# Attention and a gated FFN on one core: weights decoded in pieces of 512 columns, the ninth transposed block in the scores' banks, scores ranked further ahead

## The chip, the cores and the metric

The kernel runs on one core of one Trainium2 chip. The metric is device time in microseconds. Before the change three runs took 1001.59 to 1005.19 us, with a median of 1004.27. The core has five engines that work side by side, each through its own instructions in their order: TensorE (PE in the profile), VectorE (DVE), ScalarE (ACT), GpSimd (POOL) and SyncE (SP), which issues the transfers. PE writes its results into PSUM, which has eight banks; each holds 512 float32 columns.

## What is computed

For 8 batches of 576 tokens, attention with 8 heads of 64 columns, in which scores more than tau under their row's maximum are dropped, and then an FFN whose hidden layer is gated by a convolution of three taps along the tokens:

```python
scores = scale * np.matmul(q, k.transpose(0, 1, 3, 2))
thresh = np.max(scores, axis=-1, keepdims=True) - tau
scores = np.where(scores >= thresh, scores, -1000000000.0)
attn = softmax(scores); x = np.matmul(attn, v)      # heads side by side: [8, 576, 512]
h = np.maximum(x @ w_in, 0.0)                       # [8, 576, 1024]
conv_out[:, s] = sum(conv_w[k] * h[:, s + k - 1] for k in range(3))
out = (h * 1.0 / (1.0 + np.exp(-conv_out))) @ w_out # [8, 576, 512]
```

The FFN's weights (w_in 512 x 1024, w_out 1024 x 512, conv_w 3 x 1024) come as 64-bit floats and are turned into pairs of 32-bit floats on the chip, a high and a low part.

## The kernel before

**Tiles.** A batch is worked on in two chunks: tokens 0 to 255 (query tiles 0 and 1 of 128 rows) and 256 to 575 (tiles 2 and 3 of 128 rows, tile 4 of 64). Heads go in pairs, four pairs a chunk. One query tile of one pair is a unit; in `unit` (L403) PE makes the scores of each head into a score buffer `ps_s` of two PSUM banks, 288 of 512 columns used in each (L423 for batch 0, in plain float32 and 64 rows; L434 for the others, with q and k split in high and low parts). DVE takes the row maximum (L443, `few`), ACT the exponential (L449, `em`), DVE masks and sums (L452), and after a few operations on single columns POOL normalises (L482). The 64-row tile has both heads in one buffer. There are two score buffers, so a batch makes 36 turns of them: 16 in its first chunk, 20 in its second.

`transposes` (L487) turns the two heads' 1152 columns in nine blocks of 128 on PE (L504): four, four and one, each group into a bank of `ps_t`, of which there are two, and ACT copies it out to `eT` (L498). The 64-row tile makes a group of four and one of two halves (L528). `attend` (L541) multiplies by v, also in a `ps_t` bank, and splits the result in a high part on ACT (L558) and a low one on DVE (L561). `mm1` (L567) and `mm2` (L636) are the FFN: 8 blocks of hidden columns per chunk (L580 on PE into `ps_w`; relu L595 on ACT, the taps L598 on POOL and L607 on DVE, the gate L616 and L614, and split into the ring `gh`, `gl` at L624 and L253), and output tiles of 128 tokens (L645). `ps_w` has two banks, which makes 4 + 2 + 2 = 8.

**Weights.** `split` (L268) decodes a piece of 128 rows and `WN` = 256 columns: a transfer on SP (L306), the absolute value of the upper words on ACT (L279), four operations on DVE (a clamp L283, a shift L287, then sign and low bits joined at L291 and L295), the high part by ACT (L298) and the low part by POOL (L253). There are 32 pieces, 16 for each weight, and they lie in the `ot` buffers, two in all. Batch 0's attention runs while they are decoded.

**What sets the order.** Nothing is issued directly. `op` (L64) records an operation with its engine, a planned duration, the parts of buffers that it reads and writes, and a rank: the number of the unit it belongs to, less `AHEAD` of its kind ('s' for the steps of `unit`, 't' for transposes, 'a' for attend, 'prep' for q, k and v, 'w' for weights, of which `WRATE` pieces are ranked per unit). FFN work has no lead. `Plan.run` (L82) then plays the program with the planned durations, and on each engine always takes the ready operation of lowest rank; on PE it may pass over some within `KEEP` ranks to avoid a change of kind. The order in which it takes them is the order of the program. The dependences that the plan knows are those of the named parts (`r=` and `w=`). The semaphores of the program are put in afterwards, by a layer that looks at what each instruction reads and writes: for PSUM it orders accesses to one tensor by bank.

Of the kernel before, what the change touches and what calls it, by code (L numbers as in the profile page):

```python
# [18 lines left out]
AHEAD = {'s': 4.5, 't': 4.0, 'a': 3.5, 'prep': 5.5, 'w': 2.0}  # L19
# [4 lines left out]
BACKLOG = {'pool': 10000.0, 'dve': 500.0, 'act': 9e9}  # L24
WRATE = (1.75, 1.25)
ALT = 3.0

# [6 lines left out]
KEEP = 0.6  # L34


class Buf:
# [6 lines left out]
    def __getitem__(self, key):  # L44
        if self.tile is None:
            self.tile = self.pool.tile(self.shape, self.dtype, tag=self.tag, bufs=self.bufs, name=self.name)
        return self.tile[key]

# [146 lines left out]
def tile_tau_attention_gated_ffn(  # L195
# [3 lines left out]
    kd: bass.AP,  # L199
    vc: bass.AP,  # L200
# [19 lines left out]
    GROUPS = [(0, 1), (2, 3, 4)]  # L220
    CHUNKS = [(0, 255), (255, 321)]
    COLS = [(0, 256), (254, 322)]
    NEW = [(0, 256), (256, 320)]
# [4 lines left out]
    ps_s = ctx.enter_context(tc.tile_pool(name="ps_s", bufs=2, space=PSUM))  # L228
# [11 lines left out]
    op("sp", 100, lambda: nc.sync.dma_start(tau_sb[:], tau.broadcast_to([P, 1])), w=[(tau_sb, 0)], ahead=100.0)  # L240

# [26 lines left out]
    def split(src, n, name, high, low, hr, lr):  # L268


        tmp = plan.buf(wk, "ot", 2, [P, 3 * WN], U32, name)

        def view(dtype=F32):
            words = tmp[:, :2 * n].rearrange("p (f two) -> p f two", two=2)
            return [x.bitcast(dtype) for x in (words[:, :, 0], words[:, :, 1], tmp[:, 2 * n:3 * n])]

        def f1():
            lo, hi, a = view()
            nc.scalar.activation(a, hi, AF.Abs)  # L279

        def f2():
            a = view()[2]
            nc.vector.tensor_scalar(a, a, TINY, None, op0=ALU.max)  # L283

        def f3():
            a = view(U32)[2]
            nc.vector.tensor_scalar(a, a, 3, 0x3FFFFFF8, op0=ALU.logical_shift_left, op1=ALU.bitwise_and)  # L287

        def f4():
            lo, hi, a = view(U32)  # L290
            nc.vector.scalar_tensor_tensor(a, hi, 0xC0000000, a, op0=ALU.bitwise_and, op1=ALU.bitwise_or)  # L291

        def f5():
            lo, hi, a = view(U32)
            nc.vector.scalar_tensor_tensor(a, lo, 29, a, op0=ALU.logical_shift_right, op1=ALU.bitwise_or)  # L295

        def f6():
            nc.scalar.activation(high(), view()[2], AF.Copy)  # L298

        def f7(engine):  # L300
# [481 lines left out]
```

## Time and profile before

| what | value |
| --- | --- |
| median of three runs | 1004.27 us |
| the profiled execution's own time | 1007.23 us |
| its span, first to last instruction | 1005.4 us |
| mean granted PE clock | 0.974 |
| busy: PE, DVE, POOL, ACT | 948.6, 816.0, 725.6, 706.4 us |
| transfers | 77.76 MB, mean 77 GB/s |

The page has busy times for the whole span, and these hide stages. It also has the span in forty slices; other views group instructions by line and form (busy time, mean duration of one, idle time before them and who ended it), list who waited for whom (us in total, how often, the longest), and give each engine's busy time in chosen stretches. A row's mean duration includes what the instruction lost to its neighbours on the chip. PE's matmuls overlap, so its busy time is not the sum of their durations.

### The profile page before, as it was taken

The numbers are of one execution on the slowest core, as the hardware profiler recorded it, in microseconds if no ns is written. First come the engines' busy times: TensorE is split into PE (matmuls) and PEld (weight loads), VectorE is DVE, ScalarE is ACT, GpSimd is POOL, SyncE is SP. The second block draws the span as 40 slices with busy tenths as digits, with TensorE's granted clock in tenths as the row PEclk, the third lists the DMA queues.
The fourth block names the chain that finished last, engine by engine and source line by source line (L and its number), as shares of the span: only waits on it lengthen the run. The fifth ranks groups of instructions, "written<-read, shape, count | busy, mean of one in ns | idle before, by whom it ended". The sixth has DMA issues, their size and how long they took to land.

```text
span 1005.4 us, 19531 instructions
## 1 busy us (share of the span) xinstructions
PE 948.6 (94%) x6368; PEld 769.7 (77%) x6368; DVE 816.0 (81%) x2023; ACT 706.4 (70%) x1575; POOL 725.6 (72%) x1157
## 2 busy tenths in 40 slices
PE   6788777999999999999999999999999999999998
PEld 3455455778888788878888888887788888887796
DVE  5889998887887967898788877898789877897543
ACT  5576676777777776777777777678776776776543
POOL 3567787687677978697776978698766886696433
PEclk9796997999999999999999999999999999999999
DMA  6434342223221233222312232213322121211000
GB/s 172 127 104 128 102 125 80 76 62 97 83 71 51 78 91 90 66 65 81 109 57 65 64 100 71 81 36 102 100 75 63 53 82 57 70 47 38 22 22 32
DMA packets 47172, 77.76 MB, mean 77 GB/s; under 512 B 5600, under 2 KB 23008, under 8 KB 47072
## 3 DMA queue, kind: packets, MB, share of 16 engines
q1 hardware_dynamic: 47072, 76.53, 26.0%
q8 instruction: 51, 0.84, 0.4%
q14 instruction: 49, 0.40, 0.1%
HBM read 67.07 MB, written 9.44 MB: 76 GB/s over the span
## 4 chain that ended last, share of the span: by engine, by line
PE 74%; DVE 8%; POOL 8%; issue 3%; ACT 3%; DMA 3%; SPq 1%; POOLq 0%; ACTq 0%; DVEq 0%
PE po L645 18%; PE ph L580 16%; PE ps_s L434 13%; PE pa L550 13%; PE ps_t L504 12%; POOL em L482 2%; POOL gl L253 2%; DVE few L443 2%; DVE em L452 2%; PE ps_s L423 1%; DMA stage<-in_w_out_dram 1%; DVE t L607 1%; POOL t L598 1%; ACT eT L498 1%; POOL ks L253 1%
## 5 line engine op out<-in xcount | busy, mean ns | idle before, releaser
L482 POOL TENSOR_SCALAR em<-em,few 128x576 f32<-128x576 f32 x288 | 259.6, 908 | 44.1 <-DVE few L477 30.5
L443 DVE TENSOR_REDUCE few<-ps_s 128x1 f32<-128x576 f32 x288 | 213.2, 750 | 67.2 <-PE ps_s L434 51.6
L580 PE MATMUL ph<-x,w1h 128*128 128x322 f32 (+1 forms) x1024 | 254.5, 311 | 1.3 <-ACT hp L595 1.0
L452 DVE SCALAR_TENSOR_TENSOR em<-ps_s,few,em 128x576 f32<-128x576 f32 x288 | 231.6, 810 | 28.6 <-ACT em L449 24.3
L449 ACT ACTIVATE em<-ps_s,few 128x576 f32<-128x576 f32 x288 | 211.8, 742 | 52.2 <-DVE few L443 43.7
L498 ACT ACTIVATE eT<-ps_t 128x512 f32<-128x512 f32 (+1 forms) x448 | 200.0, 479 | 53.7 <-PE ps_t L504 50.2
L504 PE MATMUL ps_t<-ident,em 128*128 128x128 f32 x1280 | 204.1, 282 | 18.9 <-POOL em L482 12.0
L504 PEld LDWEIGHTS ps_t<-ident,em 128*128 128x128 f32 x1280 | 154.5, 144 | 62.2 <-POOL em L482 30.1
L434 PE MATMUL ps_s<-ks,q 128*128 128x288 f32 (+1 forms) x1120 | 193.6, 307 | 6.0 <-DVE em L452 6.0
L607 DVE SCALAR_TENSOR_TENSOR t<-hp,cw,t 128x255 f32<-128x255 f32 (+1 forms) x256 | 172.7, 681 | 23.9 <-POOL t L598 20.1
L580 PEld LDWEIGHTS ph<-x,w1h 128*128 128x128 f32 x1024 | 180.1, 192 | 10.0 <-issue 3.5
L434 PEld LDWEIGHTS ps_s<-ks,q 128*128 128x128 f32 (+1 forms) x1120 | 161.1, 186 | 18.5 <-DVE em L452 6.8
L550 PE MATMUL pa<-eT,v 128*64 128x256 f32 (+1 forms) x1280 | 172.9, 417 | 1.0 <-ACT eT L498 1.0
L580 PE MATMUL ph<-x,w1l 128*128 128x322 f32 (+1 forms) x512 | 153.0, 299 | 0.1
L253 POOL TENSOR_TENSOR gl<-t,gh 128x321 fp32r<-128x321 f32 (+13 forms) x184 | 119.5, 659 | 36.0 <-ACT gh L624 33.8
L550 PEld LDWEIGHTS pa<-eT,v 128*64 128x64 f32 x1280 | 87.8, 139 | 69.8 <-issue 7.1
L645 PE MATMUL po<-w2h,gh 128*128 128x512 f32 x288 | 121.2, 421 | 2.5 <-ACT w2h L298 1.9
L645 PE MATMUL po<-w2l,gh 128*128 128x512 f32 x288 | 113.7, 395 | 0.8 <-POOL w2l L253 0.8
L645 PE MATMUL po<-w2h,gl 128*128 128x512 f32 x288 | 113.2, 393 | 0.4 <-POOL hp L590 0.3
L253 POOL TENSOR_TENSOR q<-xq,q 128x256 fp32r<-128x256 f32 (+1 forms) x112 | 93.9, 844 | 18.1 <-ACT q L391 16.8
L598 POOL TENSOR_SCALAR t<-hp,cw 128x321 f32<-128x321 f32 (+1 forms) x128 | 70.6, 553 | 45.6 <-ACT hp L595 40.5
L580 PEld LDWEIGHTS ph<-x,w1l 128*128 128x128 f32 x512 | 98.2, 192 | 0.9 <-POOL w1l L253 0.3
(54 smaller groups left out, 1115.8 us busy)
## 6 DMA issues: line engine op xcount, KB each, us to landing
v<-in_vc_dram SPq DMA_DIRECT2D x64, 320.0 KB, 2.9
out_dram<-ot SPq DMA_DIRECT2D x36, 256.0 KB, 2.1
xk<-in_kd_dram SPq DMA_DIRECT2D x28, 320.0 KB, 3.0
xq<-in_qd_dram SPq DMA_DIRECT2D x56, 160.0 KB, 2.2
xk<-in_kd_dram SPq DMA_DIRECT2D x28, 288.0 KB, 2.9
xq<-in_qd_dram SPq DMA_DIRECT2D x56, 128.0 KB, 2.1
stage<-in_w_in_dram SPq DMA_DIRECT2D x16, 256.0 KB, 3.1
stage<-in_w_out_dram SPq DMA_DIRECT2D x16, 256.0 KB, 2.6
```

The costliest lines, as they stand in the source:

```text
L253: engines[e].tensor_tensor(dst, x, y, op=ALU.subtract)
L434: nc.tensor.matmul(ps[:(r + 1) * n, c, :CH], lhsT=qt[j][i][:, o - r * n:o + n], rhs=kt[j][:, at:at + CH], start=(i == 0), stop=(i == 1))
L443: nc.vector.tensor_reduce(few[:rows, nm], ps[:rows, :, :CH], op=ALU.max, axis=mybir.AxisListType.XY, negate=True)
L449: nc.scalar.activation(view(), ps[:rows, :, :CH], AF.Exp, bias=few[:rows, nm])
L452: nc.vector.scalar_tensor_tensor(view(), ps[:rows, :, :CH], few[:rows, th], view(), op0=ALU.is_ge, op1=ALU.mult, accum_out=few[:rows, total])
L482: engines[e].tensor_scalar(sl, sl, few[:rows, 6 + h:7 + h], few[:rows, 8 + h:9 + h], op0=ALU.mult, op1=ALU.add)
L498: "act", act(w, True), lambda dst=dst, src=src: nc.scalar.activation(dst(), src(pt), AF.Copy),
L504: nc.tensor.transpose(out=pt[:, i * P:(i + 1) * P], in_=em[:, (b0 + i) * P:(b0 + i + 1) * P], identity=ident[:])
L550: nc.tensor.matmul(pa[j * D:(j + 1) * D, :w], lhsT=vt[:, blk + j, :], rhs=eT[:, blk, :w], start=(r == 0), stop=(r == 4))
L580: nc.tensor.matmul(ph[:, :an], lhsT=w1[w][:, cb, fs], rhs=xs[cb][:, h, :an], start=(cb == 0 and i == 0), stop=(cb == NCB - 1 and i == 2))
L607: nc.vector.scalar_tensor_tensor(t[:, :kn], hp[:, k:kn + k], cw[:, 3 * f + k:3 * f + k + 1], t[:, :kn], op0=ALU.mult, op1=ALU.add)
L645: nc.tensor.matmul(po[:], lhsT=x[:, f, at:at + P], rhs=w[:, f, :], start=(f == 0 and i == 0), stop=(f == NFB - 1 and i == 2))
```

## The change

- **Weights.** `WN` is 512: 16 pieces, 8 for each weight. The 64-bit words land in one of four buffers shared with the keys (`ks`), the values in one of two shared with the low parts of q (`q2`). The clamp goes to POOL, with DVE as the other choice; DVE keeps three operations. The first three loads are issued by ACT's queue, at the program's start. `WRATE` is 0.99 and 0.812 pieces a unit.
- **Odd blocks.** The ninth block of a tile, and the two halves of the 64-row tile, go into the last 128 columns of a bank of a score buffer, units alternating over the two buffers and then over their banks. The two score buffers are now made once and stay; the planner keeps a part's name for the scores and one for each bank's free columns, so to the plan the two uses are independent.
- **Order.** `AHEAD` is 6.0 for scores (4.5), 3.25 for transposes (4.0), 4.5 for prep (5.5), 3.0 for weights (2.0), and a load of weights has 5.5 more; `KEEP` is 1.2 (0.6). The first output tile's products are ranked with chunk 0's.
- **Smaller ones.** Batch 0's keys come for both heads of a pair in one transfer of 128 rows x 640 columns, loaded again for the second chunk, and scaled by one ACT operation. ACT's table is loaded by a first exponential of a column of zeros at the program's start. Later keys of both heads lie in one buffer, `ks`, four in all.

```diff
-AHEAD = {'s': 4.5, 't': 4.0, 'a': 3.5, 'prep': 5.5, 'w': 2.0}
+AHEAD = {'s': 6.0, 't': 3.25, 'a': 3.5, 'prep': 4.5, 'w': 3.0, 'load': 5.5}
-WRATE = (1.75, 1.25)
+WRATE = (0.99, 0.812)
+EARLY = 1
-KEEP = 0.6
+KEEP = 1.2
...
+    warm = const("warm", [P, 1], F32)
+    op("pool", 100, lambda: nc.gpsimd.memset(warm[:], 0.0), w=[(warm, 0)], ahead=200.0)
+    op("act", 1300, lambda: nc.scalar.activation(warm[:], warm[:], AF.Exp), w=[(warm, 0)], ahead=200.0)
...
-    def split(src, n, name, high, low, hr, lr):
-        tmp = plan.buf(wk, "ot", 2, [P, 3 * WN], U32, name)
+    def split(src, n, name, high, low, hr, lr, queue="sp"):
+        stage = plan.buf(wk, "ks", 4, [P, KW], U32, name)
+        value = plan.buf(wk, "q2", 2, [P, 2, QW], U32, f"{name}_f")
...
-        def f2():
-            a = view()[2]
-            nc.vector.tensor_scalar(a, a, TINY, None, op0=ALU.max)
+        def f1(e):
+            engines[e].tensor_scalar(v(), v(), TINY, HUGE, op0=ALU.max, op1=ALU.min)
...
+        op(queue, 450, load, w=[hi, lo], ahead=w + (AHEAD["load"] if queue == "sp" else 90))
+        op("act", act(n), f0, w=[a], r=[hi], ahead=w)
+        op("pool", n * 1.69 + 80, f1, w=[a], ahead=w, other=[("dve", 150 + n * 0.65)])
+        op("dve", 150 + n * 0.55, f2, w=[a], ahead=w)
+        op("dve", 150 + n * 1.1, f3, w=[a], r=[hi], ahead=w)
+        op("dve", 150 + n * 1.1, f4, w=[a], r=[lo], ahead=w)
...
-    WN = 256
+    WN = 512
...
+    scores = [plan.buf(ps_s, f"ps_s{i}", 1, [P, 2, 512], F32, f"ps_s{i}") for i in range(2)]
+    taken = collections.Counter()
+    def turns(what, n):
+        taken[what] += 1
+        return (taken[what] - 1) % n
...
+        op("sp", 450, lambda: nc.sync.dma_start(ks[:], kp[p]), w=[(ks, 0)], ahead=a + 2)
+        op("act", act(S + D), lambda: nc.scalar.activation(ks[:], ks[:], AF.Copy, scale=0.125), w=[(ks, 0)], ahead=a)
...
-            ps = plan.buf(ps_s, "ps_s", 2, [P, 2, 512], F32, f"ps_s_{u}_{h}")
+            ps = scores[turns("s", 2)]
...
-            pt = plan.buf(ps_t, "ps_t", 2, [P, 512], F32, f"ps_t_{u}_{i}")
             width = sum(w for w, _, _ in evacs)
+            if width > P:
+                pt = plan.buf(ps_t, "ps_t", 2, [P, 512], F32, f"ps_t_{u}_{i}")
+                part, bank = (pt, 0), lambda: pt
+            else:
+                at = turns("t", 4)
+                pt, half = scores[at % 2], at // 2
+                part, bank = (pt, 1 + half), lambda: pt[:, half, 512 - P:]
```

**DVE, the weights in batch 0.** Rows of DVE's order in batch 0's first chunk before the change, where two pieces of w_in (`stage`) stand between the maximum of a head and the masks of its unit (`few` holds the columns of maxima, limits and sums, `em` the exponentials):

```order
L443 TENSOR_REDUCE few_319<-ps_s_1_340 128x1
L283 TENSOR_SCALAR stage_286<-stage_286 128x256
L283 TENSOR_SCALAR stage_310<-stage_310 128x256
L287 TENSOR_SCALAR stage_286<-stage_286 128x256
L287 TENSOR_SCALAR stage_310<-stage_310 128x256
L291 SCALAR_TENSOR_TENSOR stage_286<-stage_286 128x256
L291 SCALAR_TENSOR_TENSOR stage_310<-stage_310 128x256
L295 SCALAR_TENSOR_TENSOR stage_286<-stage_286 128x256
L295 SCALAR_TENSOR_TENSOR stage_310<-stage_310 128x256
L452 SCALAR_TENSOR_TENSOR em_350,few_319<-ps_s_0_306,few_319,em_350 128x576
```

And DVE's order in the same chunk after it (`stage_105` the words of a piece, `stage_f` the values; `ps_s_127` and `ps_s_136` are the two score buffers from here on):

```order
L473 TENSOR_REDUCE few_303<-ps_s_127 128x1
L473 TENSOR_REDUCE few_303<-ps_s_136 128x1
L476 TENSOR_SCALAR few_303<-few_303,tau_sb 128x1 x2
L325 SCALAR_TENSOR_TENSOR stage_f<-stage_105,stage_f 128x512
L482 SCALAR_TENSOR_TENSOR em_319,few_303<-ps_s_127,few_303,em_319 128x576
L482 SCALAR_TENSOR_TENSOR em_319,few_303<-ps_s_136,few_303,em_319 128x576
L328 SCALAR_TENSOR_TENSOR stage_f<-stage_105,stage_f 128x512
L507 RECIPROCAL few_303<-few_303 128x2
```

Between a unit's last maximum and its first mask stood eight operations of 256 columns, and now one of 512; the pieces' operations are spread between those of the softmax, and the clamp is gone from DVE.

**PE, the odd block in batch 3.** Rows of PE's order before the change, with the semaphores that each waits for: a unit's blocks five to eight, three products of an output tile (`po`), and the ninth block in a `ps_t` bank of its own, ahead of the next scores:

```order
L504 MATMUL ps_t_4_4782<-ident,em_4669 128x128 [waits Pool_49]
L504 MATMUL ps_t_4_4782<-ident,em_4669 128x128 x3
L645 MATMUL po_4754<-w2h,gh 128x512
L645 MATMUL po_4754<-w2h,gl 128x512
L645 MATMUL po_4754<-w2l,gh 128x512
L504 MATMUL ps_t_8_4799<-ident,em_4669 128x128 [waits Activation_49]
L434 MATMUL ps_s_1_4801<-ks_1_1_3826,q_3_1_1_0_4484 128x288 [waits DVE_49]
```

And PE's order after it, at about the same place: the last of a head's scores into `ps_s_136`, eight blocks of one unit, the ninth block of the next unit (`em_4707`) into a bank of that same `ps_s_136`, and FFN products (`ph`) behind it:

```order
L465 MATMUL ps_s_136<-ks_0_3424,q_28_4531 128x288
L540 MATMUL ps_t_0_4778<-ident,em_4636 128x128 [waits PE_49]
L540 MATMUL ps_t_0_4778<-ident,em_4636 128x128 x3
L540 MATMUL ps_t_4_4786<-ident,em_4636 128x128 [waits DVE_49]
L540 MATMUL ps_t_4_4786<-ident,em_4636 128x128 x3
L540 MATMUL ps_s_136<-ident,em_4707 128x128 [waits DVE_49,Pool_49]
L615 MATMUL ph_1_4793<-x_3624,w1h 128x322
```

The ninth block waited for ACT, which empties `ps_t`; now it may stand ahead of its unit's other blocks, and it waits for DVE, whose newest instruction before it in the program reads the scores in that buffer.

More of the change, by code (lines that the diff above doesn't have):

```diff
@@ L1 @@
+import collections
 import heapq
@@ L47, in __getitem__ @@
         return self.tile[key]
+Chunk = collections.namedtuple("Chunk", "b tiles new cols tokens done")
 class Plan:
@@ L289, in f4 @@
         def f4():
[L290 to L300, printed above, removed]
-            subtract(engine, low(), view()[2], high().bitcast(F32))
-        lo, hi, a = ((tmp, i) for i in range(3))
@@ L316, in tile_tau_attention_gated_ffn @@
+        op("act", act(n), lambda: nc.scalar.activation(high(), v(), AF.Copy), w=[hr], r=[a], ahead=w)
+        op(
+            "pool", pool(n), lambda e: subtract(e, low(), v(), high().bitcast(F32)), w=[lr], r=[a, hr], ahead=w,
+            other=[("dve", dve(n))]
+        )
+    WN = 512
+    KW, QW = 2 * S + D, max(c.new[1] for c in chunks)
     n3 = 3 * NFB
```

221 lines of the change are left out of this document (114 added, 107 removed).

## The prediction

> **What bounds the kernel now.** I read the page first, then busy time by stage, then what PE waits for in the early and in the late part. The page's rows of engines and of forty slices (one digit each, 25 us a slice):
>
> ```profile
> PE 948.6 (94%) x6368; PEld 769.7 (77%) x6368; DVE 816.0 (81%) x2023; ACT 706.4 (70%) x1575; POOL 725.6 (72%) x1157
> PE   6788777999999999999999999999999999999998
> DVE  5889998887887967898788877898789877897543
> PEclk9796997999999999999999999999999999999999
> ```
>
> PE is the busiest engine, but in its first seven slices it is not full, and there DVE shows the nines; the granted clock falls to 0.6 and 0.7 in the same slices. So there are two stages with different limits. I cut the span where the max reductions begin for batch 0's second half (56.0), batch 1 (135.8), batch 1's second half (189.2), batch 2 (262.8), batch 7 (839.4), and at the last head (942.0), and asked for busy time in these stretches:
>
> ```profile
> core 0: us, PE busy (x) PEld busy (x) DVE busy (x) ACT busy (x) POOL busy (x), PEclk, DMA share, GB/s
> 0.00:56.00 56.00, 38.57 (x202) 21.99 (x202) 39.59 (x108) 33.04 (x68) 25.13 (x50) 0.88 0.50 141
> 56.00:135.80 79.80, 63.23 (x381) 41.28 (x379) 74.30 (x187) 55.74 (x127) 58.50 (x84) 0.85 0.40 117
> 135.80:189.20 53.40, 41.39 (x252) 30.72 (x253) 47.20 (x124) 37.42 (x83) 42.01 (x62) 0.87 0.33 99
> 189.20:262.80 73.60, 72.11 (x493) 60.02 (x493) 60.63 (x143) 54.22 (x119) 57.03 (x84) 1.00 0.25 72
> 262.80:839.40 576.60, 571.44 (x3976) 478.64 (x3973) 480.93 (x1195) 430.15 (x955) 446.38 (x704) 1.00 0.26 75
> 839.40:942.00 102.60, 102.60 (x742) 86.71 (x741) 87.03 (x221) 71.07 (x163) 72.71 (x128) 1.00 0.16 50
> ```
>
> Up to 189.2 us PE idles 17.4 + 16.6 + 12.0 = 46.0 us; from there to 942 only 1.5 + 5.2 + 0 = 6.7 us. DVE is busy 93% of the second stretch (74.30 of 79.80) and 88% of the third, against 83% in the long one. What PE waits for up to 189.2, largest first:
>
> ```profile
> PE ps_s L423 <- DVE em L452: 11.4, 10, 3.0
> PE ps_t L504 <- POOL em L482: 8.5, 11, 1.1
> PE ps_s L423 <- ACT ks L364: 6.1, 1, 6.1
> PE ps_s L434 <- DVE em L452: 5.2, 3, 3.1
> ```
>
> Scores wait until DVE has masked the previous head of their bank, and transposes until POOL has normalised. From 189.2 to 942 the same view is nearly empty, and it is complete:
>
> ```profile
> PE ps_t L504 <- POOL em L482: 3.5, 6, 1.6
> PE ps_t L504 <- DVE x L561: 1.1, 1, 1.1
> PE ps_s L434 <- DVE em L452: 0.8, 2, 0.6
> PE po L645 <- ACT hp L595: 0.6, 1, 0.6
> PE po L645 <- POOL hp L590: 0.3, 1, 0.3
> ```
>
> So the early part is bound by DVE, which decodes weights between softmaxes; the rest by PE, where each new wait of PE is paid in full. The profiled execution took 1007.23 us with a span of 1005.4; the median of the timed runs is 1004.27. I make the sum as a difference and take it off the median, 2.96 us under the profiled time.
>
> **Part 1: weights in 512 columns.** DVE's largest groups in the first 200 us, the four decode lines among them:
>
> ```profile
> L452 DVE SCALAR_TENSOR_TENSOR em<-ps_s,few,em 128x576 f32<-128x576 f32 x54 | 43.1, 808 | 1.8 <-ACT em L449 1.3
> L443 DVE TENSOR_REDUCE few<-ps_s 128x1 f32<-128x576 f32 x56 | 41.6, 749 | 18.8 <-PE ps_s L423 14.5 <-PE ps_s L434 4.2
> L295 DVE SCALAR_TENSOR_TENSOR stage<-stage 128x256 uint32<-128x256 uint32 x32 | 18.8, 591 | 0.0
> L291 DVE SCALAR_TENSOR_TENSOR stage<-stage 128x256 uint32<-128x256 uint32 x32 | 17.2, 539 | 0.0
> L283 DVE TENSOR_SCALAR stage<-stage 128x256 f32<-128x256 f32 x32 | 14.2, 445 | 4.8 <-ACT stage L279 4.8
> L287 DVE TENSOR_SCALAR stage<-stage 128x256 uint32<-128x256 uint32 x32 | 13.5, 425 | 0.0
> L607 DVE SCALAR_TENSOR_TENSOR t<-hp,cw,t 128x255 f32<-128x255 f32 x16 | 10.2, 645 | 0.0
> L607 DVE SCALAR_TENSOR_TENSOR t<-hp,cw,t 128x321 f32<-128x321 f32 x7 | 5.0, 718 | 0.5 <-POOL t L598 0.5
> ```
>
> Now DVE pays 18.8 + 17.2 + 14.2 + 13.5 = 63.7 us. Afterwards there are 16 pieces with three operations each: the clamp (L283's work) goes to POOL. No row has 512 columns of these kinds. At most each costs twice its 256-column row: 16 x 2 x (591 + 539 + 425) = 49.8 us. At least the two with two inputs cost the mask's row scaled, 808 x 512/576 = 718 ns, and the shift stays at 425: 16 x 1861 = 29.8 us. I take the slope of L607, (718 - 645)/66 = 1.1 ns a column, so 283 ns more for each: 16 x (874 + 822 + 708) = 38.5 us. DVE is relieved of 25 us (14 to 34). It is busy 91% over the second and third stretch but 71% in the first, and a wait for PE or ACT sits between its operations; I let 0.8 of it reach the end: **-20 us** (-11 to -27), which the 46.0 us of idle PE has room for.
>
> What pays for it on the other engines:
>
> ```profile
> L482 POOL TENSOR_SCALAR em<-em,few 128x576 f32<-128x576 f32 x54 | 49.5, 923 | 9.9 <-DVE few L477 3.9 <-DVE few L446 3.8 <-PE ps_s L434 1.7
> L253 POOL TENSOR_TENSOR w2l<-stage,w2h 128x256 fp32r<-128x256 f32 x16 | 12.3, 770 | 2.6 <-ACT w2h L298 2.5
> L253 POOL TENSOR_TENSOR w1l<-stage,w1h 128x256 fp32r<-128x256 f32 x16 | 12.2, 764 | 5.4 <-ACT w1h L298 5.2
> L253 POOL TENSOR_TENSOR ks<-xk,ks 64x576 fp32r<-64x576 f32 x5 | 7.4, 1471 | 0.4
> L449 ACT ACTIVATE em<-ps_s,few 128x576 f32<-128x576 f32 x55 | 40.5, 741 | 15.1 <-DVE few L443 15.1
> L498 ACT ACTIVATE eT<-ps_t 128x512 f32<-128x512 f32 x54 | 31.7, 595 | 9.5 <-PE ps_t L504 9.3
> L369 ACT ACTIVATE xk<-xk 128x640 f32<-128x640 f32 x6 | 4.4, 728 | 0.2 <-POOL w2l L253 0.2
> ```
>
> POOL gets 16 clamps of about 923 x 512/576 = 820 ns, 13 us; its 32 subtractions (24.5 us) become 16 of about 767 + (1471 - 767) x 256/320 = 1330 ns, 21 us. That is +10 us on an engine with 21 us of idle time in the second stretch alone (58.50 of 79.80 busy): hidden. Without that cover it delays the normalising that transposes wait for (a rival below). ACT does 32 passes of 595 ns for 64 shorter ones, and batch 0's keys are scaled once a pair and chunk at 728 ns; ACT has idle time in every stretch. SP issues 16 weight loads for 32 and 8 key loads for 16, so nothing behind them in its queue starts later for their number: 0.
>
> **Part 2: the odd block in the scores' banks.** A query tile has nine blocks of 128 columns; the ninth (two halves of 64 for the last tile) is copied out by these rows of the whole run:
>
> ```profile
> L498 ACT ACTIVATE eT<-ps_t 128x128 f32<-128x128 f32 x128 | 35.6, 278 | 2.5 <-PE ps_t L504 2.1
> L498 ACT ACTIVATE eT<-ps_t 128x64 f32<-128x64 f32 x32 | 7.1, 223 | 0.4 <-PE ps_t L528 0.3
> ```
>
> These 160 no longer take a turn of the two ps_t banks; they lie in a bank with a head's scores, which three operations read: maximum 749 ns, exponential 741, mask 808. The order on PE shows what follows: the odd block waits on DVE where it stood behind ACT's copies or POOL alone, and the next FFN products are queued behind it on PE. In the new plan this wait has no price. Its price from rows: the five batches of the long stretch hold 180 heads in 576.6 us, 3.2 us a head, so a score buffer, of which there are two, turns every 6.4 us; its readers fill 2.3 of these, 36%. An odd block that arrives at any time meets a reader with that chance and waits half of it, 0.38 us: 0.14 us a block. After 189.2 us, 236 of 288 heads are left, so 131 odd blocks: 18 us, and 22 for all 160. The lower end is 0, if the blocks come when the buffer is idle. I take **+12 us**, nearer to the upper end because the rows quoted ahead of the diff have the odd block of one tile only eight transposes behind scores into its own bank. Nothing before 189.2 is charged: PE idles there anyway. ACT and DVE wait for each other in these banks too, under ACT's 25% and DVE's 17% of idle time in the long stretch: 0, at most what a rival below charges.
>
> The Trainium skill (PSUM — Partial Sum Buffer, section on PSUM bank collisions) says to guard PSUM by bank and quadrant and not by address. By that rule free columns are no free buffer, and the term is nearer to 22 than to 0; no run shown so far has two uses in one bank.
>
> **Part 3: scores further ahead, steadier PE.** With scores ranked 6.0 tiles ahead and the ps_t banks freed of the odd blocks, PE's 6.3 us of waits from 189.2 to 942 can go, at most all: **-3 us** (0 to -6).
>
> **Part 4: the first microseconds.** The first scores wait 6.1 us for scaled keys (L364). Three weight loads now go out on ACT's queue at once, and ACT takes the absolute values of the first piece before the first keys:
>
> ```profile
> L364 ACT ACT_TABLE_LOAD x1 | 1.3, 1283 | 4.3 <-DMA ks<-in_kd_dram 4.3
> stage<-in_w_in_dram SPq DMA_DIRECT2D x16, 256.0 KB, 3.1
> ```
>
> The table load leaves the path (-1.3 us). A 512 KB load lands after at most 2 x 3.1 us; 0.6 us of absolute values and 0.7 of scaling follow: 7.5 to 8.1 instead of 6.1. **+1 us** (-1 to +2).
>
> Sum: -20 + 12 - 3 + 1 = -10 us: 997 for the profiled execution, **994 us** for the median. With all ends together: -34 and +13.
>
> **The rivals.**
> Slower: PE's new waits eat the gain. An odd block that finds its bank in use waits for a whole reader, because that reader itself starts late on DVE: 0.36 x 0.77 = 0.28 us a block, 36 us for 131 blocks: -20 + 36 - 3 + 1 = +14, 1018 us. For it speaks that PE is full at 99% after 189.2; against it, that scores run further ahead, so PE has other work ranked before the odd block. It decides from (20 + 3 - 1)/131 = 0.17 us a block. Chance 0.20. The Trainium skill's rule in part 2 speaks for this case.
> No change: POOL's clamps stand in front of the normalising. If each of the 16 (0.82 us) delays transposes that now wait 8.5 us for POOL, 13 us of the 20 are lost: -10 + 13 = +3, 1007 us. Against it: POOL's 27% of idle time. Chance 0.22.
> Far faster: DVE saves 34 us, all of it reaches the end, and the odd blocks find idle banks: -34 - 3 + 1 = -36, 968 us. For it: 46.0 us of idle PE and a clock at 0.85 to 0.88 in those stretches. Against it: DVE's softmax alone remains near full. Chance 0.13.
>
> **How the numbers follow.** My forecast has 0.45. A measurement of this kernel can tell about 0.5%, 5 us, from no change; faster is forecast plus far faster, 0.58, same 0.22, slower 0.20. The range is that of the ends, 970 to 1018: it leaves out part of the far faster case and the upper half of the slower one.
>
> **What would show it.** Right: the three decode rows on DVE sum to some 38 us; PE's idle time before batch 1's second half falls from 46.0 to under 30; from there to the last head PE's waits grow from 6.7 to some 15 us, on the odd blocks' rows, with DVE and ACT as releasers. Wrong: decode rows near 50 us; PE waiting 22 us or more on odd blocks; or transposes that wait for POOL's em more than 8.5 us early on.

## The result, and the profile after

| | before | after |
| --- | --- | --- |
| median | 1004.73 us (4 runs, 1001.59 to 1007.02) | 1026.26 us (4 runs, 1025.90 to 1027.25) |
| ratio, with 95% interval | | 1.0221 [1.0205, 1.0237] |
| the profiled execution | 1007.23 us | 1025.90 us |
| its span | 1005.4 us | 1024.1 us |

The change made the kernel 2.2% slower. The forecast was 994 us, and the range ended at 1018. The page's rows of engines and slices after the change, to be laid beside those of before:

```profile
PE 952.7 (93%) x6368; PEld 769.0 (75%) x6368; DVE 796.8 (78%) x1927; ACT 704.4 (69%) x1544; POOL 758.8 (74%) x1174
...
PE   4867879999999999999999999999999999999998
...
DVE  5877887997878788887886788797787878887443
...
POOL 4789888988767886697766876698765977677333
PEclk9988879999999999999999999999999999999999
```

DVE has 19 us less to do and POOL 33 us more. PE's first slices are no fuller than before, and from the eighth on the digits show nothing: a loss of 3% inside a nine is not visible there. The same cuts as before (first maxima of batch 0's second half, batch 1, its second half, batch 2, batch 7, and the last head) give busy times by stage, with the columns of the view shown of before:

```profile
0.00:57.50 57.50, 36.55 (x207) 21.66 (x207) 39.77 (x93) 32.16 (x60) 36.35 (x55) 1.00 0.54 179
57.50:144.40 86.90, 65.11 (x388) 42.74 (x388) 70.35 (x155) 53.83 (x110) 77.77 (x86) 0.83 0.28 87
144.40:189.50 45.10, 40.74 (x259) 32.11 (x259) 37.70 (x92) 35.10 (x75) 37.78 (x51) 0.86 0.35 104
189.50:251.60 62.10, 60.08 (x423) 48.40 (x424) 53.22 (x138) 48.51 (x107) 53.72 (x81) 1.00 0.28 84
251.60:846.90 595.30, 579.47 (x3990) 480.90 (x3988) 477.97 (x1177) 432.62 (x959) 449.34 (x716) 1.00 0.25 74
846.90:957.00 110.10, 107.77 (x753) 90.68 (x753) 90.95 (x229) 76.09 (x172) 79.06 (x138) 1.00 0.16 48
```

Two things went another way than forecast. Up to 189.5 us PE idles 20.95 + 21.79 + 4.36 = 47.1 us, as much as before (46.0), and in the second stretch it is POOL that is nearly full: 77.77 of 86.90, 89%. And the five middle batches take 595.3 us where they took 576.6.

A better measure than the cuts is how far the work of PE has come, since scores run further ahead after the change. I gave each matmul the median distance between the end of its predecessor and its own end for its kind and shape, and read off when each profiled execution had done the same share of that work. In us against the kernel before (minus is ahead of it):

| share of PE's work | 2% | 9% | 15% | 30% | 50% | 90% | all |
| --- | --- | --- | --- | --- | --- | --- | --- |
| time of the kernel before | 40.1 | 135.7 | 213.7 | 353.1 | 539.0 | 910.5 | 1001.7 |
| after | +1.0 | +0.3 | -5.8 | +0.4 | +7.3 | +17.4 | +18.7 |
| ninth blocks back in their own bank | +5.6 | +0.4 | -6.4 | -6.0 | -7.5 | -8.6 | -8.5 |
| before, with only the ninth blocks moved | -1.1 | -1.7 | -1.7 | +5.4 | +10.6 | +25.2 | +27.3 |
| after, clamp on DVE | -2.4 | -6.5 | -14.2 | -8.2 | -0.3 | +10.0 | +11.3 |
| the best version | -1.1 | -10.4 | -19.1 | -17.6 | -19.4 | -19.8 | -19.7 |

The change gains 5.8 us while weights are decoded, and then loses 24.5 us, some in every part of the work that follows. (The rows below the second are experiments.) The columns up to 15% depend on the weight that batch 0's matmuls are given: with one median for each form, taken from the kernel before, the changed kernel is 3.7 us ahead at 15%, the one with ninth blocks back 5.7 and the best version 18.0. From 30% on the two ways agree within 1.3 us. Each row is one execution, and that of the kernel with ninth blocks back is the slowest of its four (998.73 us).

**The early part.** What PE waits for up to 189.5 us, largest first (us in total, times, longest):

```profile
PE ps_t L540 <- POOL em L512: 15.9, 13, 2.5
PE ps_s L454 <- ACT ks L391: 9.8, 1, 9.8
PE ps_s L454 <- DVE em L482: 7.7, 8, 2.3
PE ps_t L540 <- DVE x L597: 3.4, 3, 2.3
```

Scores wait for DVE's masks 7.7 us in batch 0, where they waited 11.4, and transposes wait for POOL's normalising 15.9 us, where they waited 8.5. The groups of the first 200 us show why (line, engine, operation, form, count, busy us, mean ns, idle before):

```profile
L512 POOL TENSOR_SCALAR em<-em,few 128x576 f32<-128x576 f32 x54 | 51.5, 962 | 3.5 <-PE ps_t L540 1.5 <-DVE few L507 0.9 <-DVE few L476 0.4
L319 POOL TENSOR_SCALAR stage_f<-stage_f 128x512 f32<-128x512 f32 x16 | 31.2, 1949 | 7.1 <-ACT stage_f L316 6.7
L325 DVE SCALAR_TENSOR_TENSOR stage_f<-stage,stage_f 128x512 uint32<-128x512 uint32 x16 | 13.9, 866 | 0.0
L328 DVE SCALAR_TENSOR_TENSOR stage_f<-stage,stage_f 128x512 uint32<-128x512 uint32 x16 | 12.8, 799 | 0.0
L322 DVE TENSOR_SCALAR stage_f<-stage_f 128x512 uint32<-128x512 uint32 x16 | 9.2, 576 | 3.1 <-POOL stage_f L319 3.0
```

DVE's three operations take 13.9 + 12.8 + 9.2 = 35.9 us (priced 38.5). The clamp on POOL takes 1949 ns (priced 820) and 31.2 us in all, in front of the normalising that transposes wait for.

**The late part.** From 189.5 to 957 us most of what the view of waits has is new: 13.6 of its 18.7 us are the ninth blocks (`ps_s L540`, and `ps_s L564` for the halves). The largest rows:

```profile
PE ps_s L540 <- ACT em L479: 6.1, 12, 0.9
PE po L680 <- POOL gl L280: 3.5, 4, 1.0
PE ps_s L540 <- DVE em L482: 2.7, 6, 0.7
PE ps_t L540 <- POOL em L512: 1.6, 3, 0.9
PE ps_s L540 <- DVE few L473: 1.5, 5, 0.4
```

The three readers of a score bank are all there: exponential (ACT L479), mask (DVE L482) and maximum (DVE L473). With four smaller rows the waits of ninth blocks sum to 13.6 us, about half of what is lost. Much of the rest sits inside PE's busy time: 579.47 us in the middle batches against 571.44, for the same matmuls. The readers themselves run no slower: maximum, exponential and mask take 753, 741 and 814 ns there, and took 750, 743 and 811 before. So what PE loses is waiting, and not time in slower accesses to a shared bank. Because the view of waits misses a part, I also added up, over the five middle batches, the distances from the end of each matmul to the end of the one before, by kind:

| us in the five middle batches | stretch | blocks of 128, ninth ones in it | halves | scores | all else |
| --- | --- | --- | --- | --- | --- |
| before | 576.6 | 97.3 | 5.0 | 110.7 | 363.6 |
| ninth blocks back | 574.9 | 94.0 | 5.3 | 108.5 | 367.1 |
| after | 595.3 | 107.8 | 7.0 | 112.7 | 367.8 |
| before, ninth blocks moved | 599.8 | 110.9 | 6.5 | 116.9 | 365.5 |
| after, planner with held banks | 586.0 | 97.1 | 6.1 | 115.9 | 366.9 |

Between the second and the third row everything else is equal to 0.7 us. The 20.4 us lie on the blocks (+13.8), the halves (+1.7) and the scores (+4.2). A ninth block alone is 307 ns behind its predecessor on average, and 110 in the median: 0.20 us a block is waiting.

**The start.** The timeline of the first microseconds after the change (start, duration, engine):

```profile
7.92 0.33 ACTq L313 DMA_DIRECT2D stage<-in_w_in_dram  x1
...
8.98 0.72 ACT L391 ACTIVATE ks<-ks 128x640 f32<-128x640 f32 x1
...
9.75 1.46 PEld L454 LDWEIGHTS ps_s<-ks,q 64*128 64x128 f32 x8 [9.75 <-ACT ks L391]
```

The first keys are issued at 1.62 us and land 6.2 us later. ACT's queue issues its third load only then, at 7.92 us, ACT takes two absolute values, and the keys are scaled at 8.98. The first scores start at 9.75 us (6.1 before; 7.5 to 8.1 forecast). By 2% of the work 1.0 us of that is left.

### The profile page after: what moved, and what is told of

Read it like the earlier page. It is cut to its first block, busy times and chain, and to the rows that moved or that the text cites. A ratio compares the mean times of both kernels' runs of the same rounds, so it can differ in the third digit from the quotient of the medians.

```text
span 1024.1 us, 19301 instructions
## 1 busy us (share of the span) xinstructions
PE 952.7 (93%) x6368; PEld 769.0 (75%) x6368; DVE 796.8 (78%) x1927; ACT 704.4 (69%) x1544; POOL 758.8 (74%) x1174
## 4 chain that ended last, share of the span: by engine, by line
PE 65%; POOL 16%; DVE 9%; ACT 5%; issue 5%; DMA 1%; SPq 0%; POOLq 0%; ACTq 0%; DVEq 0%
PE po L680 15%; PE ph L615 14%; PE pa L586 13%; PE ps_s L465 12%; PE ps_t L540 8%; POOL em L512 4%; POOL gl L280 3%; DVE few L473 3%; DVE em L482 2%; ACT em L479 2%; POOL stage_f L319 2%; PE ps_s L540 2%; POOL q L280 1%; POOL ks L280 1%; POOL t L633 1%
## 5 line engine op out<-in xcount | busy, mean ns | idle before, releaser
L473 DVE TENSOR_REDUCE few<-ps_s 128x1 f32<-128x576 f32 x288 | 213.7, 752 | 89.3 <-PE ps_s L465 62.6
L482 DVE SCALAR_TENSOR_TENSOR em<-ps_s,few,em 128x576 f32<-128x576 f32 x288 | 231.0, 814 | 44.8 <-ACT em L479 20.8
L615 PE MATMUL ph<-x,w1h 128*128 128x322 f32 (+1 forms) x1024 | 250.7, 308 | 0.4 <-ACT ot L687 0.2
L479 ACT ACTIVATE em<-ps_s,few 128x576 f32<-128x576 f32 x288 | 209.5, 742 | 52.3 <-DVE few L473 33.7
L540 PE MATMUL ps_t<-ident,em 128*128 128x128 f32 x1152 | 170.2, 280 | 21.7 <-POOL em L512 17.5
L534 ACT ACTIVATE eT<-ps_t 128x512 f32<-128x512 f32 x288 | 166.6, 598 | 21.3 <-PE ps_t L540 20.1
L540 PEld LDWEIGHTS ps_t<-ident,em 128*128 128x128 f32 x1152 | 135.4, 143 | 57.2 <-POOL em L512 25.2
L280 POOL TENSOR_TENSOR gl<-t,gh 128x321 fp32r<-128x321 f32 (+13 forms) x184 | 119.5, 662 | 16.0 <-ACT gh L659 13.6
L680 PE MATMUL po<-w2h,gh 128*128 128x512 f32 x288 | 117.8, 409 | 0.0
L280 POOL TENSOR_TENSOR q<-xq,q 128x256 fp32r<-128x256 f32 (+1 forms) x112 | 96.1, 865 | 10.1 <-ACT eT L534 6.4
```

What stands on the lines that cost most here:

```text
L280: engines[e].tensor_tensor(dst, x, y, op=ALU.subtract)
L473: nc.vector.tensor_reduce(few[:rows, nm], ps[:rows, :, :CH], op=ALU.max, axis=mybir.AxisListType.XY, negate=True)
L479: nc.scalar.activation(view(), ps[:rows, :, :CH], AF.Exp, bias=few[:rows, nm])
L482: nc.vector.scalar_tensor_tensor(view(), ps[:rows, :, :CH], few[:rows, th], view(), op0=ALU.is_ge, op1=ALU.mult, accum_out=few[:rows, total])
L534: "act", act(w, True), lambda dst=dst, src=src: nc.scalar.activation(dst(), src(bank()), AF.Copy),
L540: nc.tensor.transpose(out=pt[:, i * P:(i + 1) * P], in_=em[:, (b0 + i) * P:(b0 + i + 1) * P], identity=ident[:])
```

## The experiments

The theory after the result: the ninth blocks in the score banks cost some 0.2 us each from batch 1 on, and POOL's slow clamp ate most of the gain of the wide weights. The rival for the late loss: the new order numbers keep PE badly fed. Ratios are against the kernel before, run in turn on the same chip; for the change itself it is 1.0221.

**Ninth blocks back** in the transposes' own buffers, all else as changed:

```diff
-            if width > P:
+            if True:
                 pt = plan.buf(ps_t, "ps_t", 2, [P, 512], F32, f"ps_t_{u}_{i}")
```

> The changed kernel with one part undone: the ninth blocks of transposes take their turn of the two ps_t banks again; weights, order numbers and all else stay changed. Theory (the ninth block's waits for the readers of its bank are what PE loses after batch 2): about 20 us come back, 1006 us (1000 to 1012), and PE has no waits on ps_s for transposes any more. Rival (the order numbers are what costs: scores 6.0 ahead and KEEP 1.2 starve the FFN, seen in po's waits for gl): the time stays at 1020 to 1027.

Measured: 994.67 us (991.82 to 998.73), ratio 0.9897 [0.9859, 0.9934]. The middle batches, and all that PE waits for from batch 1's second half (186.5 us) to the last head (929.3):

```profile
247.90:822.80 574.90, 569.73 (x3984) 478.85 (x3983) 481.31 (x1203) 430.49 (x961) 447.54 (x696) 1.00 0.26 77
```

```profile
PE po L680 <- POOL gl L280: 3.9, 4, 1.0
PE ps_t L540 <- DVE x L597: 0.7, 2, 0.5
PE ps_t L540 <- POOL em L512: 0.5, 2, 0.3
PE ps_s L465 <- DVE em L482: 0.3, 1, 0.3
```

The late loss is gone, and so are its rows; the wait for `gl` is here as well, so it does not come from the sharing. One line is worth 31.6 us, and the rest of the change is a gain. I had expected 1006: the price of the sharing was higher than I still thought.

**Only the ninth blocks**, put into the kernel before: two fixed score buffers, and the ninth blocks in their free columns, with the old numbers, weights and loads.

```diff
-            ps = plan.buf(ps_s, "ps_s", 2, [P, 2, 512], F32, f"ps_s_{u}_{h}")
+            ps = scores[turns("s", 2)]
...
+            if width > P:
+                pt = plan.buf(ps_t, "ps_t", 2, [P, 512], F32, f"ps_t_{u}_{i}")
+                part, bank = (pt, 0), lambda: pt
+            else:
+                at = turns("t", 4)
+                pt, half = scores[at % 2], at // 2
+                part, bank = (pt, 1 + half), lambda: pt[:, half, 512 - P:]
```

> The kernel before with that part alone: the two score buffers stay, the ninth blocks lie in their free columns, all numbers and the weights as before. Theory: 1004 + 18 = 1022 us (1014 to 1030), PE waits on the ninth blocks' rows with DVE and ACT as releasers, some 0.17 us a block or more. Rival: 1004 us, within 5, since with the old numbers the order has the scores' readers done by then.

Measured: 1034.66 us, ratio 1.0293 [1.0264, 1.0322]. What PE waits for from batch 1's second half (192.3 us) to the last head (970.8):

```profile
PE ps_s L517 <- ACT em L456: 3.8, 10, 0.6
PE ps_s L517 <- DVE em L459: 3.7, 10, 1.1
PE ps_t L517 <- POOL em L489: 3.3, 7, 1.1
PE ps_s L441 <- DVE em L459: 2.8, 4, 1.4
```

The same releasers appear in a kernel that has nothing else of the change, and 29 us, a little above the range expected and near the 31.6 of the other direction. So this part alone is enough for the loss; the medians show no share that comes from meeting the other parts. The two fixed buffers don't cost it: the version with ninth blocks back has them too.

**Order numbers back** to 4.5, 4.0 and 5.5 with `KEEP` 0.6, all else as changed:

```diff
-AHEAD = {'s': 6.0, 't': 3.25, 'a': 3.5, 'prep': 4.5, 'w': 3.0, 'load': 5.5}
+AHEAD = {'s': 4.5, 't': 4.0, 'a': 3.5, 'prep': 5.5, 'w': 3.0, 'load': 5.5}
-KEEP = 1.2
+KEEP = 0.6
```

> The changed kernel with the lead of scores, transposes and prep and KEEP as before (4.5, 4.0, 5.5, 0.6); weights and ninth blocks stay changed. Theory: the waits for the ninth blocks' banks remain, at most 5 us of change, 1021 to 1028 us. Rival (the numbers are what costs): back to about 1006 us.

Measured: 1030.26 us, ratio 1.0248 [1.0224, 1.0273]. The rival falls: the new numbers are a gain of some 3 to 4 us, if anything, as forecast in part 3. (The numbers for weights stayed new; the version with ninth blocks back has all the new numbers and no late loss.)

**The clamp on DVE**, without a choice between the two engines, all else as changed:

```diff
-        op("pool", n * 1.69 + 80, f1, w=[a], ahead=w, other=[("dve", 150 + n * 0.65)])
+        op("dve", 150 + n * 0.55, lambda: f1("dve"), w=[a], ahead=w)
```

> The changed kernel with the weights' clamp back on DVE, where it costs 16 x about 0.6 = 10 us, while POOL loses 16 x 1.95 = 31 us. Theory (POOL, 89% busy from 57 to 144 us, is what holds the early part): 8 us faster than the changed kernel, 1018 us, and transposes wait less than 10 us for POOL's em ahead of batch 1's second half (15.9 now). Rival (DVE is still the bound there): same as the changed kernel or up to 5 us slower.

Measured: 1018.23 us, ratio 1.0126 [1.0096, 1.0156], as expected. The row of the clamp in the first 200 us, and the wait of transposes for POOL up to 189.5 us, which was 15.9:

```profile
L319 DVE TENSOR_SCALAR stage_f<-stage_f 128x512 f32<-128x512 f32 x16 | 9.5, 592 | 0.0
```

```profile
PE ps_t L540 <- POOL em L512: 7.3, 8, 2.0
```

592 ns on DVE against 1949 on POOL for the same operation on the same data. Giving DVE 9.5 us back gains 8 us, though DVE was the engine to be relieved.

**Maximum alone.** On the version with ninth blocks back, the clamp on POOL without its upper bound, so without the minimum with 3e38 (which matters for infinite weights only):

```diff
-            engines[e].tensor_scalar(v(), v(), TINY, HUGE, op0=ALU.max, op1=ALU.min)
+            engines[e].tensor_scalar(v(), v(), TINY, None, op0=ALU.max)
```

> The changed kernel with ninth blocks back in the transposes' buffers, and the clamp on GpSimd made with one operation (maximum alone, without the minimum, as the kernel before has it on the vector engine). Theory 1: the two operations are what makes the clamp 1.95 us; with one it takes 0.9 to 1.1 us, GpSimd is freed of 14 us in the stretch where it is 89% busy, and the time falls by 3 to 6 us from 994.7. Theory 2: a maximum over 512 columns is slow on GpSimd whatever else is asked: it stays near 1.9 us and the time at 994 to 995.

Measured: 992.94 us, ratio 0.9884 [0.9861, 0.9906], not to be told from 0.9897. The clamp's row:

```profile
L319 POOL TENSOR_SCALAR stage_f<-stage_f 128x512 f32<-128x512 f32 x16 | 24.1, 1506 | 3.4 <-ACT stage_f L316 3.2
```

Neither theory fits well. The second operation costs 0.44 us of 1.95, and the maximum alone is still two and a half times DVE's clamp. Not all that POOL does is as slow: the normalising, a multiplication and an addition over 576 columns, takes 962 ns there. The 16 clamps of the changed kernel take 1915 to 2148 ns, so the neighbours of the moment explain little of it. The two rows also differ in their second operands, constants in the clamp and one value a partition in the normalising, and no run separates that from the operation. The Trainium skill (GPSIMD Engine Reference, section on engine selection) advises VectorE for an elementwise maximum, and calls work with one input on GpSimd roughly line-rate. The two rows of the clamp, 1949 and 592 ns, do not bear the second part out.

**First loads on SP's queue**, ninth blocks back:

```diff
-            src[c * P:(c + 1) * P, f], WN, f"stage_{i}", h, l, *((x, (c, f.start)) for x in dst), "act" if i < 3 else "sp"
+            src[c * P:(c + 1) * P, f], WN, f"stage_{i}", h, l, *((x, (c, f.start)) for x in dst), "sp"
```

> The changed kernel with ninth blocks back in the transposes' buffers and the first three weight loads on SyncE's queue in place of the scalar engine's. Theory: the first maximum comes at about 7.5 to 8.5 us instead of 11.5, but the lost 4 us lie ahead of a stretch that GpSimd's clamps bound, so most of it is lost again by 9% of the matmul work: 992 to 995 us against 994.7. Rival: the start shifts everything after it: 990 to 991.

Measured: 991.09 us (986.97 to 993.49), ratio 0.9873 [0.9840, 0.9907]; the first maximum comes at 10.7 us (11.6 with these loads on ACT's queue), not at 7.5 to 8.5. ACT's queue was therefore only a part of what held the start. The keys' transfer is the rest: its 320 KB land 5.9 us after their issue here, which comes 1.0 us later, behind two loads of weights, and in 6.2 in the changed kernel. The first row is of the changed kernel's first 14 us, the second of its whole run:

```profile
ks<-in_kp_dram SPq DMA_DIRECT2D x2, 320.0 KB, 6.2
```

```profile
v<-in_vc_dram SPq DMA_DIRECT2D x64, 320.0 KB, 2.9
```

Transfers of the same size take 2.9 us as a median of the run, so the size alone does not make it; before the change the first keys came in 88 KB pieces that landed in 2.5. What has changed beside them is the traffic: 3.83 MB in the first 14 us, at 273 GB/s, where it was 2.29 MB at 164. Runs with smaller pieces, or without the weight loads beside them, weren't made. On the end the loads do nothing that this measurement can show.

**Half of the ninth blocks** in the score banks, those of every second unit back in their own:

```diff
-            if width > P:
+            if width > P or u % 2:
```

> The changed kernel with the ninth blocks of every second unit back in the transposes' own buffers, the others still in the score banks. Theory A (each sharing costs its own wait, about 31.6 us over 160 blocks, 0.2 us a block): half the blocks, half the cost, about 1010 us, 1007 to 1014. Rival (a threshold: the transposes' own buffers are short, so half the relief already costs nothing, or half the sharing already costs all): 997 or less, or 1020 or more.

Measured: 1011.64 us, ratio 1.0077 [1.0058, 1.0096]. 994.67, 1011.64, 1026.26: the first 80 blocks cost 17.0 us and the second 14.6. That is a price per block, near 0.2 us, and no threshold.

**A planner that knows, first attempt:** the ninth block and its copy are given the part of the buffer that the scores have.

```diff
-                part, bank = (pt, 1 + half), lambda: pt[:, half, 512 - P:]
+                part, bank = (pt, 0), lambda: pt[:, half, 512 - P:]
```

> The changed kernel, with the planner told what the program enforces: a ninth block writes the same part of the score buffer as the scores, and its copy reads that part. Nothing else differs. Theory A (the sharing itself costs: a bank now serves scores, their three readers, a ninth block and its copy one after the other, and no order can make that shorter than the readers' 2.3 us and the copy's wait): most of the 30 us stay, 1012 to 1026 us. Theory B (the sharing is cheap, the loss comes from an order made without knowing of it): 1000 us or less, near the 994.7 of the kernel with its ninth blocks back in their own bank.

Measured: 1326.40 us, ratio 1.3203. What PE waited for, the three largest of the span:

```profile
PE ps_s L465 <- DVE em L482: 57.1, 25, 2.6
PE ps_s L465 <- ACT eT L534: 51.8, 70, 1.7
PE ps_t L540 <- POOL em L512: 45.1, 60, 2.5
```

This answers another question than the one I asked. The planner keeps users of one part in the order in which they were recorded, and there the next unit's scores stand behind this unit's ninth block. So scores could hardly run ahead any more: they wait for the copy of the ninth block (`eT`) 70 times. It prices this order, and says nothing of theory A or B.

**A planner that knows, second attempt.** A score buffer is held, by scores until their three readers are done or by a ninth block until its copy is; whoever is ready first takes it. Scores also claim `em` and ninth blocks `eT` when they are issued. Control: these claims alone.

```diff
-                    ):
+                    ) and (not self.locks[i] or holder.get(self.locks[i][0], self.locks[i][1]) == self.locks[i][1]):
...
+                if self.locks[pick]:
+                    bank, owner, count = self.locks[pick]
+                    holder[bank] = owner
+                    rest.setdefault(owner, count)
...
-                "pe", 480 if q2 is None else 532 * len(js), mm, w=[(ps, 0)],
+                "pe", 480 if q2 is None else 532 * len(js), mm, w=[(ps, 0), (em, h)],
```

> The changed kernel with a planner that treats each score buffer as held: by scores until their maximum, exponential and mask are done, or by a ninth block until its copy is done; whoever comes first takes it (the earlier attempt to tell the planner had fixed the recorded order of holders, and so kept scores from running ahead, 1326 us). Scores and ninth blocks also claim the buffers that their results go to, so that nobody holds a bank while waiting for those. Theory A (a bank's turn with a fifth and sixth user is simply longer, whatever the order): 1015 to 1030 us. Theory B (the loss is the planner's blindness): 995 to 1005.

> Control for the planner with held buffers: the changed kernel with the same earlier claims of the result buffers, without the holding. If the claims alone do nothing, 1024 to 1028 us, as the changed kernel; if they delay scores (they take the buffer of the masked scores about 1 us earlier), up to 1035.

Measured: 1019.43 us, ratio 1.0150 [1.0135, 1.0165]; the control 1028.93, ratio 1.0246 [1.0231, 1.0262]. The middle batches with held banks:

```profile
264.00:850.00 586.00, 574.03 (x3974) 477.58 (x3973) 483.46 (x1182) 432.03 (x957) 448.42 (x709) 1.00 0.26 75
```

Knowing is worth 9.5 us against the control (whose claims cost 2.7), and 24.8 us to the version without sharing remain. In the middle batches about half of the loss stays: 586.0 us, between the 595.3 of the changed kernel and the 574.9 without sharing. The table of distances shows what happened there: ninth blocks nearly stop waiting (blocks of 128 take 97.1 us instead of 107.8) and scores wait instead (115.9 against 112.7, and 108.5 without sharing). So the time is in theory A's range, and in these batches the order mostly chose who waits. That a bank's longer turn is the cause of all that remains isn't shown: this is one rule, first come, first served, and the rest of the 24.8 us lies outside the middle batches, which the table doesn't cover.

**The copy on DVE**, so that the bank's readers sit on fewer engines:

```diff
-                    "act", act(w, True), lambda dst=dst, src=src: nc.scalar.activation(dst(), src(bank()), AF.Copy),
+                    *(("act", act(w, True), lambda dst=dst, src=src: nc.scalar.activation(dst(), src(bank()), AF.Copy)) if width > P
+                      else ("dve", dve(w), lambda dst=dst, src=src: nc.vector.tensor_copy(dst(), src(bank())))),
```

> The changed kernel with the copies of the ninth blocks (100 of 277 and 227 ns in the five middle batches) made by the vector engine instead of the scalar engine, still from the score banks. In the changed kernel the scalar engine stands idle 22.2 + 5.2 us before these copies in the middle batches, and the vector engine 10.7 us before maxima until such a copy is done. Theory C (the loss runs through two readers' engines that hold each other up in the shared bank, and PE is late because of that): the vector engine makes maximum, mask and copy in its own order, the waits between the two engines go, 1010 to 1019 us. Theory D (what counts is PE's own wait for the bank's readers, whoever copies): 1022 to 1030; the vector engine also gets 26 us more work, 3% of the span, which lies under its idle 17%.

Measured: 1041.03 us (1037.90 to 1042.67), ratio 1.0350 [1.0304, 1.0395]. The middle batches, and the row of the copies in them:

```profile
256.30:861.20 604.90, 584.05 (x3995) 483.35 (x3995) 497.56 (x1280) 418.64 (x864) 455.81 (x723) 0.99 0.25 73
```

```profile
L535 DVE COPY eT<-ps_s 128x128 f32<-128x128 f32 x80 | 22.3, 286 | 31.4 <-PE ps_s L465 18.6 <-PE pa L587 6.1 <-PE ps_s L541 3.6
```

The time is far above C's range and above D's: the copies stand in DVE's order 31.4 us waiting for PE, and the masks and maxima queued behind them wait too. Bringing the readers together on one engine doesn't pay here. But the run replaced one wait by another, so it doesn't show how much the two reading engines cost by holding each other up; which of the waits in a bank's turn (ninth block behind the readers, or next scores behind the copy) weighs how much in another order stays open.

**The best version:** ninth blocks back, clamp on DVE, first loads on SP's queue.

> The changed kernel with three edits: ninth blocks back in the transposes' own buffers, the clamp of the weights on the vector engine, the first three weight loads on SyncE's queue. If the costs found so far add up, from 994.7 us: the clamp's move was worth 8 us on the changed kernel, the earlier start up to 3.5 us, so 983 to 987 us, and the lead over the kernel before stands at 15% of the matmul work already (-15 us or more) and does not melt. If the clamp's move pays only where the ninth blocks also wait (rival), 990 to 995.

Measured: 986.79 us (984.43 to 987.51), ratio 0.9818 [0.9795, 0.9841]: 1.8% under the kernel before, with an interval below that of the version with ninth blocks back alone, and in the range expected. The clamp's move is worth 4.3 us here (against 991.09, the same with the clamp on POOL), not the 8 that I had put in. Its second stretch and its middle batches:

```profile
51.20:133.50 82.30, 65.17 (x402) 41.79 (x401) 75.95 (x166) 55.22 (x116) 63.48 (x80) 0.88 0.33 104
...
235.90:811.70 575.80, 570.34 (x3987) 479.16 (x3986) 480.81 (x1203) 432.39 (x963) 451.21 (x700) 1.00 0.26 77
```

POOL is down from 89% to 77% in the second stretch, DVE is the fullest again at 92%, and the lead of 19.1 us at 15% of the work is kept to the end.

## Why the prediction was wrong

**Part 2 is the step that failed: its size.** The mechanism stood there (a semaphore wait on the readers, FFN products queued behind it, no price in the plan), and so did the place, batch 1's second half onward: at 15% of PE's work the changed kernel and the one with ninth blocks back differ by 0.6 us (2.0 by the other weights). I priced a block at 0.14 us, charged 131, got 18 and took 12 of it. The runs give 27.2 us between the two profiled executions and 31.6 between the medians: 0.17 to 0.20 us a block over all 160, and 0.21 to 0.24 over the 131. Three things were missing. The wait is longer than half a reader: in the middle batches 32 of 81 ninth blocks of 128 columns end more than 0.05 us later than the median distance, a chance of 0.40 where I had 0.36, and they do so by 0.50 us on average, where I had 0.38. With this goes that a bank is taken for longer than its readers run: from the start of the maximum to the end of the mask of a head go 3.2 us on average in the middle batches (the n-th maximum against the n-th mask), not the 2.3 of the three durations. The trace of the kernel before has the same 3.2, so I could have read it there. The scores lose 4.2 us in the middle batches, where I had 0: they wait 1.7 us for copies of ninth blocks, and 3.6 us for masks, where it is 1.5 without the sharing. And the discount from 18 to 12 had nothing behind it but a lower bound of 0; the rule of the Trainium skill (PSUM — Partial Sum Buffer, section on PSUM bank collisions) that stands beside it pointed to the upper end, and the runs went past that.

**Part 1 was right in what it counted on DVE** (35.9 us against 38.5) and wrong in what it called hidden. The clamp was priced from the normalising row, scaled by columns, at 820 ns; it took 1949, so POOL got 31.2 us instead of 13. The subtractions came as priced (11.0 + 10.7 us). Of the -20 us 5.8 are there at 15% of the work. How much of the rest the clamp took is known only roughly: by medians 8.0 us on the changed kernel, and 4.3 between the best version and the same with the clamp on POOL, whose runs spread over 6.5 us. The best version's lead of 19.1 us at 15% looks like the -20, but that is luck: with the clamp on DVE its four operations take 46.8 us of the 63.7 they took before, so DVE saves 16.9 us and not 25, and parts 3 and 4 are in that lead too. No run has the wide weights alone, so what they are worth by themselves stays open.

**The rivals were added up wrongly.** I set the slower case (PE's new waits) and the case of no change (POOL's clamps) side by side, as if one excluded the other. They are different mechanisms in different stages, and both came. Single edits lead from the best version to the changed kernel: 986.79 us, with the clamp on POOL 991.09, with the first loads on ACT's queue 994.67, with ninth blocks in the score banks 1026.26. The steps are +4.3, +3.6 (no more than the spread of these runs) and +31.6, where my sum had 0, +1 and +12. The slower rival's price (0.28 us a block) was too high, its turning point (0.17) was passed.

**What it would show** had one test that failed to warn: PE waiting 22 us or more on ninth blocks. The view of waits shows 13.6 us, because much of the wait is inside PE's busy time. Other signs were sound: early idle time 47.1 us, not under 30; PE's idle time from there to the last head 20.2 us, not some 15; and transposes waiting 15.9 us for POOL.

**Parts 3 and 4.** Part 3 has its -3: 2 to 4 us by the numbers put back and by the version with ninth blocks back, which gains 2.1 us after 15%. Part 4 missed the start by 1.7 us: it timed a load of weights and ACT's work, and left out that the keys themselves land only at 7.8 us (1.62 + 6.2), with 1.2 us of ACT's queue on top. Whether the late start reached the end the medians can't tell (3.6 us, inside their spread).

## What to carry to other kernels

Free columns of a PSUM bank were not a free buffer here: the program orders a second use behind the readers of the first, at about 0.2 us a use, and a planner that knew of it won back 7 to 9.5 us of some 30. Price a moved operation from a row of the same operation on the engine it goes to; a row of another operation, scaled by size, was off by 2.4. And where two rivals sit in different stages, add them.

## What the hardware showed that I had not expected

- A clamp (maximum and minimum, 128 x 512 float32) took 1949 ns on POOL and 592 to 747 on DVE; a maximum alone 1506 on POOL, while multiply and add over 576 columns took 962 there.
- In the run of 1326 us, in which PE was busy 83% of the span (1103.77 of 1325.90 us), its granted clock over the span was 0.876; the other profiled executions had 0.97 to 0.99. What sets it isn't shown.
- Transfers of 320 KB landed in 6.2 us at the start, beside 512 KB weight loads, and in a median of 2.9 over the run.
